# A spectral layer beside a Mish MLP: a shorter reciprocal root on VectorE, and a few tiles and reductions in other slots

## The chip, the cores and the metric

One core of a Trainium2 chip runs the whole program. The metric is device time in microseconds of one execution. TensorE (PE) multiplies matrices into PSUM, VectorE (DVE) and ScalarE (ACT) work on rows, GpSimd (POOL) does some of the subtractions, and SyncE (SP) issues the transfers.

## The reference, cut to what matters

```python
x = A_x                                   # (1, 2048, 512)
xn = layernorm(x)                         # eps 1e-5
X = rfft2(xn) * (w_r + 1j * w_i)          # spectral branch
y = irfft2(X, s=(2048, 512))
h = xn @ w1 + b1                          # w1: 512 x 1792
act = h * tanh(softplus(h))               # Mish
out = x + y + act @ w2                    # w2: 1792 x 512
```

## The kernel before

The 2048 rows are cut into four groups of 512 rows, each of four blocks of 128 (block s of group g is called (g, s) here). Every matrix operand is split into a high and a low half of 16 bits, and a product is three matmuls (`mm3`: high by high, high by low, low by high; lines 86, 89, 90).

The MLP runs in half tiles. There are 56 tiles (g, f), four groups by 14 columns of 128. An *up tile* (`mlp_up`, PSUM tile `ph`, line 725) is twelve matmuls; ScalarE then applies Mish (`hb`, line 733), and ScalarE and VectorE split the result into halves (`a`, lines 334 and 335). A *down tile* (`mlp_down`, PSUM tiles `pa`) is twelve matmuls that add one tile to the group's four sums. After a group's 14 down tiles `mlp_end` reads the four sums out (`m`, line 779), which frees their PSUM for the next group's. `mlp_all` decides the order: as long as there are fewer than `lag` up tiles ahead of the down tiles, an up tile comes next, otherwise a down tile.

The spectral branch normalises each group (`stats`: line 176 to 180, then the reciprocal root `rsqrt_of`, then `norm`), transposes its blocks (`transpose`: tile `pt`, line 200, copied to `xnT` by VectorE in line 290 and ScalarE in line 291), and makes the first transform (`s1_forward`: `psS`, a butterfly `bt_s` on VectorE, a cast `y` on ScalarE and a subtraction on GpSimd, line 129). The result goes to DRAM and comes back turned (`p2_unit`, `psP`). Four spectra follow (`spectrum`): each has two pairs of PSUM tiles `psD` (`d_pair`), the product with the weights, and `psA`, `psT` with a second butterfly `bt_t`. `s1_inverse` (`psY`) ends it.

Tiles `pt` and `ph` share one pool of two PSUM buffers, in the order in which they are made. The spectral tiles `psS`, `psP`, `psD`, `psA`, `psT` and `psY` share another pool of two. The largest weight of the spectral product is found by eight reductions of 128 x 1024 and one of `w0` (`prep_spectral`, lines 458 and 467), then GpSimd takes the maximum over the partitions (`am`), and a scale `sc_u` is made of it.

Three tables set the order. Ahead of the stream there are numbered slots: each holds some pieces of work, and after each slot one half tile is issued. Then comes the stream of spectral work: each piece carries a weight, and half tiles are issued in proportion to the sum of weights (`B_END` and `N_WGT`). At last the 16 inverse blocks are spread over the half tiles left. A scheduler orders the instructions of neighbouring pieces by their priority, so that an engine's queue is not exactly the order of the code.

```python
lag = LEAD if sc["ahead"] else LAG
for k in range(13, 23):
    slots[k].append((next, maxima, None))
while done[0] - start < used * (B_END - start) / N_WGT and half_tile():
```

Of the kernel before, what the change touches and what calls it, by code (L numbers as in the profile page):

```python
# [19 lines left out]
P = 128  # L20
NS2 = 16
NFC = F // P
CONST_SCALE = 1024.0
LAG = 4
NA = 5
HB = 3
LEAD = 8
E_UP = 11
N_WGT = 117.6
B_END = 98  # L30
T_LAG = 4
T_HOLD = 2
# [7 lines left out]
def spectral_mlp_kernel(ctx, tc, x, wt, w0, w1, b1, w2, cT, cIT, cM, out):  # L40
    nc = tc.nc
# [3 lines left out]
    sp = ctx.enter_context(tc.tile_pool(name="sp", bufs=1))  # L45
# [96 lines left out]

    def rsqrt_of(g, ve):

        eng = nc.gpsimd if g else nc.vector
        r = sp.tile([P, 4], F32, tag="rr", name=f"rr_{g}_0", bufs=4)

        eng.tensor_scalar(
            r.bitcast(I32), ve.bitcast(I32), -0.5, float(0x5F3759DF), op0=ALU.mult, op1=ALU.add
        )  # L150
        for k in range(3):

            t = sp.tile([P, 4], F32, tag="rt", name=f"rt_{g}_{k}", bufs=2)
            eng.tensor_mul(t, r, r)
            q = sp.tile([P, 4], F32, tag="rq", name=f"rq_{g}_{k}", bufs=2)
            if g:

                eng.tensor_mul(q, t, ve)
                eng.tensor_scalar(q, q, 0.25**k, -3.0, op0=ALU.mult, op1=ALU.add)
            else:  # L160
                eng.scalar_tensor_tensor(q, t, 0.25**k, ve, op0=ALU.mult, op1=ALU.mult)
            n = sp.tile([P, 4], F32, tag="rr", name=f"rr_{g}_{k + 1}", bufs=4)
            if g:
                eng.tensor_mul(n, q, r)
            else:
                eng.scalar_tensor_tensor(n, q, 3.0, r, op0=ALU.subtract, op1=ALU.mult)
            r = n
        rs = sp.tile([P, 4], F32, tag="rs", name=f"rs_{g}", bufs=2)
        eng.tensor_scalar(rs, r, -128.0, None, op0=ALU.mult)
        return rs  # L170

    def stats(g, ts):
# [172 lines left out]
    sc = {}  # L345
# [421 lines left out]

    def rows_back(g):

        macc[g] = cp.tile([P, 4, D], F32, tag=f"xnT{g}", name=f"m_{g}")  # L770
        nc.sync.dma_start(macc[g], xv[:, 4 * g : 4 * g + 4, :])

    def mlp_end(g):
        if g == 3:
            macc[g] = cp.tile([P, 4, D], F32, tag=f"xnT{g}", name=f"m_{g}")
        m = macc[g]
        for s in range(4):
            xr = yacc[g][s] if g == 3 else m[:, s, :]
            nc.vector.scalar_tensor_tensor(m[:, s, :], pacc[g][s], sc["out"], xr, op0=ALU.mult, op1=ALU.add)  # L779
            if g == 3:  # L780
                nc.sync.dma_start(outv[:, 4 * g + s, :], m[:, s, :])

    def mlp_all():

        tiles = [(g, f) for g in range(4) for f in range(NFC)]
        acts = {}
        up = down = n_down = 0
        while down < len(tiles):
            lag = LEAD if sc["ahead"] else LAG

            home = sc["ahead"] and up % 12 > 3
            free = down >= up - up % 4 - 8 if home else len(in_a) < NA or in_a[-NA] < down
            if free and up < len(tiles) and (up < E_UP or up - down < lag or (n_down >= 2 and up - down > lag)):
                mlp_up(*tiles[up], acts)
                if tiles[up][1] == NFC - 1 and tiles[up][0] < 3:
                    rows_back(tiles[up][0])
                up += 1
                n_down = 0
            else:
                g, f = tiles[down]  # L800
                mlp_down(g, f, acts.pop((g, f)))
                if f == NFC - 1:
# [61 lines left out]
    def stream_a():  # L864

        todo = []

        def behind(n):
            if len(todo) > n:
                ip_unit(*todo.pop(0))  # L870
                yield 1.0

        for c in range(5):
            if c < 4:
                for g in range(0, 4, 2):
                    p2_unit(c, g)
                    p2_unit(c, g + 1)
                    yield 1.6
                    yield from behind(0)
            if c:  # L880
                for g in range(4):
                    dp_unit(c - 1, g)
                    todo.append((c - 1, g))
                    yield 0.8
                    yield from behind(4)
            if c < 4:
                for wgt in spectrum(c):
# [69 lines left out]
        nc.sync.dma_start(cMt[:, :O_ID], cM[:, :O_ID])  # L957


    slots = {k: [] for k in range(24)}  # L960
    for s in range(4):
        slots[1 + s].append((s1_forward, 0, s, xh[0, s]))
    for g in range(1, 4):
        k = 6 * g - 6
        slots[k].append((st_, g))
        if g < 3:
            slots[k + 2].append((load_, g + 1))
        for s in range(4):
# [213 lines left out]
```

## Time and profile before

| | us |
|---|---|
| median of 3 runs | 400.26 (399.61 to 400.28) |
| profiled execution | 399.53 |
| its span | 397.7 |
| TensorE busy | 381.7 (96%) |
| VectorE busy | 250.8 (63%) |
| ScalarE busy | 200.9 (51%) |
| GpSimd busy | 69.7 (18%) |

The span runs from the first to the last instruction of the profiled execution. An engine that is busy 96% of it leaves little idle time; where that lies, and what ended it, is in the rows further down.

### The profile page before, as it was taken

The numbers are of one execution on the slowest core, as the hardware profiler recorded it, in microseconds if no ns is written. First come the engines' busy times: TensorE is split into PE (matmuls) and PEld (weight loads), VectorE is DVE, ScalarE is ACT, GpSimd is POOL, SyncE is SP. The second block draws the span as 40 slices with busy tenths as digits, with TensorE's granted clock in tenths as the row PEclk, the third lists the DMA queues.
The fourth block names the chain that finished last, engine by engine and source line by source line (L and its number), as shares of the span: only waits on it lengthen the run. The fifth ranks groups of instructions, "written<-read, shape, count | busy, mean of one in ns | idle before, by whom it ended". The sixth has DMA issues, their size and how long they took to land.

```text
span 397.7 us, 6578 instructions
## 1 busy us (share of the span) xinstructions
PE 381.7 (96%) x2485; PEld 191.4 (48%) x2485; DVE 250.8 (63%) x520; ACT 200.9 (51%) x325; POOL 69.7 (18%) x103
## 2 busy tenths in 40 slices
PE   8899999699998999999999999999999899999996
PEld 3444444345454454465445565455654445544442
DVE  5889777658697339843879446944439872424334
ACT  3869863576655155734646355365454474523110
POOL 0100029557565000000111101021001110220000
PEclk9999999999999999999999999999999999999999
DMA  8996015254186970353825625227471022753556
GB/s 281 363 396 258 2 53 158 81 166 151 55 297 188 271 228 3 79 134 98 255 73 144 175 54 164 77 87 200 166 190 50 27 81 70 215 171 114 173 196 253
DMA packets 49519, 61.61 MB, mean 155 GB/s; under 512 B 3776, under 2 KB 36032, under 8 KB 48848
## 3 DMA queue, kind: packets, MB, share of 16 engines
q1 hardware_dynamic: 49488, 61.20, 49.6%
q8 instruction: 19, 0.31, 0.3%
q14 instruction: 12, 0.10, 0.1%
HBM read 44.38 MB, written 16.78 MB: 154 GB/s over the span
## 4 chain that ended last, share of the span: by engine, by line
PE 54%; DVE 7%; ACT 2%; issue 2%; DMA 1%; POOL 1%; POOLq 0%; DVEq 0%; SPq 0%; ACTq 0%
PE ph L725 20%; PE pa L86 8%; PE pa L89 8%; PE pa L90 7%; PE psD L544 3%; PE psP L520 3%; DVE m L779 2%; PE psY L86 1%; PE psY L90 1%; PE psY L89 1%; PE psA L86 1%; POOL tt L129 1%; DVE a L335 1%; DMA yi<-d_t 1%; PE psA L90 1%
## 5 line engine op out<-in xcount | busy, mean ns | idle before, releaser
L725 PE MATMUL ph<-xnT,w1t 128*128 128x512 f16 x672 | 154.3, 379 | 1.9 <-ACT xnT L291 0.9
L725 PEld LDWEIGHTS <-w1t 128*128 128x128 f16 x672 | 64.7, 98 | 79.1 <-issue 2.4
L86 PE MATMUL pa<-w2r,a 128*128 128x512 f16 x224 | 84.4, 380 | 1.6 <-DVE m L779 1.4
L89 PE MATMUL pa<-w2r,a 128*128 128x512 f16 x224 | 85.0, 379 | 0.5 <-DVE w2r L335 0.5
L90 PE MATMUL pa<-w2r,a 128*128 128x512 f16 x224 | 85.0, 379 | 0.0
L335 DVE SCALAR_TENSOR_TENSOR a<-hb,sc_a,a 128x512 f16<-128x512 f32 x56 | 42.5, 761 | 56.7 <-ACT a L334 56.4
L733 ACT ACTIVATE hb<-ph,b1t,sc_exp 128x512 f32<-128x512 f32 x56 | 43.2, 771 | 59.5 <-PE ph L725 59.4
L129 POOL TENSOR_TENSOR tt<-bt_t,tt 128x512 f16<-128x512 f32 x16 | 19.6, 1230 | 195.8 <-ACT tt L128 152.9
L334 ACT ACTIVATE a<-hb,sc_a 128x512 f16<-128x512 f32 x56 | 40.1, 720 | 1.5
L90 PEld LDWEIGHTS <-a 128*128 128x128 f16 x224 | 21.9, 98 | 26.8 <-issue 1.1
L89 PEld LDWEIGHTS <-a 128*128 128x128 f16 x224 | 21.9, 98 | 25.7 <-issue 1.9
L86 PEld LDWEIGHTS <-a 128*128 128x128 f16 x224 | 21.9, 98 | 25.8 <-issue 1.2
L334 ACT ACTIVATE u<-r,sc_u 128x512 f16<-128x512 f32 x16 | 11.5, 721 | 25.3 <-DVE r L624 12.6
L129 POOL TENSOR_TENSOR y<-bt_s,y 128x512 f16<-128x512 f32 x16 | 20.1, 1261 | 18.2 <-ACT y L128 18.2
L833 DVE SCALAR_TENSOR_TENSOR m<-psY,sc_k,m 128x512 f32<-128x512 f32 x12 | 8.7, 747 | 14.9 <-PE psY L90 14.9
L128 ACT CAST tt<-bt_t 128x512 f16<-128x512 f32 x16 | 9.9, 617 | 14.9 <-DVE bt_t L126 13.4
L679 DVE SCALAR_TENSOR_TENSOR at<-psA,at 128x512 f16<-128x512 f32 x16 | 10.8, 689 | 10.4 <-ACT at L678 10.4
L128 ACT CAST y<-bt_s 128x512 f16<-128x512 f32 x16 | 9.9, 617 | 14.5 <-DVE bt_s L126 7.8
L556 ACT ACTIVATE ix<-psD 64x512 f32<-64x512 f32 x16 | 9.5, 593 | 12.8 <-PE psD L544 12.6
L678 ACT ACTIVATE at<-psA 128x512 f16<-128x512 f32 x16 | 9.2, 591 | 12.5 <-issue 7.1
L194 POOL TENSOR_TENSOR xh<-xs,xh 128x512 f16<-128x512 f32 x12 | 14.4, 1217 | 3.9 <-ACT xh L193 3.9
L544 PE MATMUL psD<-z,cMt 64*128 64x256 f16 x192 | 13.5, 270 | 1.5 <-DVE bt_t L126 1.5
(146 smaller groups left out, 510.1 us busy)
## 6 DMA issues: line engine op xcount, KB each, us to landing
wt<-in_wt_dram SPq DMA_DIRECT2D x32, 256.0 KB
x<-in_x_dram SPq DMA_DIRECT2D x8, 512.0 KB
d_y<-y SPq DMA_DIRECT2D x16, 256.0 KB
wm<-in_wt_dram SPq DMA_DIRECT2D x8, 512.0 KB
yt<-d_y SPq DMA_DIRECT2D x16, 256.0 KB
d_a<-at SPq DMA_DIRECT2D x32, 128.0 KB
ai<-d_a SPq DMA_DIRECT2D x16, 256.0 KB
d_t<-tt SPq DMA_DIRECT2D x16, 256.0 KB
```

What stands on the lines that cost most here:

```text
L86: first = nc.tensor.matmul(ps, stat(0), mov(0), start=start, stop=False)
L89: nc.tensor.matmul(ps, stat(0), mov(1), start=False, stop=False)
L90: return nc.tensor.matmul(ps, stat(1), mov(0), start=False, stop=stop)
L128: nc.scalar.copy(out[:, :, 0, :], tv)
L129: nc.gpsimd.tensor_sub(out[:, :, 1, :], tv, out[:, :, 0, :])
L194: nc.gpsimd.tensor_sub(xh[:, 1, :], xs, xh[:, 0, :])
L334: hi = nc.scalar.activation(dst_h, src, AF.Copy, scale=scale)
L335: lo = nc.vector.scalar_tensor_tensor(dst_l, src, scale, dst_h, op0=ALU.mult, op1=ALU.subtract)
L520: first = nc.tensor.matmul(ps[64 * be : 64 * be + 64, pr, k, :], yt[:, 2 * pr + be, hs, k, :], c_p2[:, k, v, hm, :], start=t == 0, stop=t ...
L544: first = nc.tensor.matmul(ps[be][:, k], c_d[rows, k0 + k, e, hs, :], z[rows, hm, 2 * (k0 + k) + e].rearrange("p g q -> p (g q)"), start=e ...
L725: last_mm = nc.tensor.matmul(ph, w1t[:, hs, dc, f * P : (f + 1) * P], xnT[g][:, hm, dc, :], start=n == 0, stop=n == 11)
L733: nc.scalar.activation(hb, ph, AF.Mish, bias=b1t[:, f : f + 1], scale=s_exp[k])
```

## The change

- The reciprocal root of a group's variances now takes eight VectorE instructions besides the one that adds the epsilon, in all four groups: a first value from the bits, one Newton step, and one step of higher order. Before, group 0 had eleven on VectorE and groups 1 to 3 had fourteen on GpSimd.
- The transposes of group 1 come one slot later, and the first up tile of group 1 (number 14 of all) waits until fewer than 6 up tiles are ahead, not 8.
- Two of the w2 splits come one slot earlier (slots 9 and 12 in place of 10 and 13).
- The ten steps of the search for the largest weight stand in slots 16 to 25 in place of 13 to 22. So there are 26 slots in place of 24, and two more half tiles are issued ahead of the stream.
- The end of a group counts 1.5 in the sum of weights, and the divisor goes from 117.6 to 120.6.

```diff
+LEAD_1 = 6
-N_WGT = 117.6
+N_WGT = 120.6
...
     def rsqrt_of(g, ve):
-        eng = nc.gpsimd if g else nc.vector
...
-        for k in range(3):
-            t = sp.tile([P, 4], F32, tag="rt", name=f"rt_{g}_{k}", bufs=2)
-            eng.tensor_mul(t, r, r)
-            q = sp.tile([P, 4], F32, tag="rq", name=f"rq_{g}_{k}", bufs=2)
-            if g:
-                eng.tensor_mul(q, t, ve)
-                eng.tensor_scalar(q, q, 0.25**k, -3.0, op0=ALU.mult, op1=ALU.add)
-            else:
-                eng.scalar_tensor_tensor(q, t, 0.25**k, ve, op0=ALU.mult, op1=ALU.mult)
...
+        v = nc.vector
+        v.tensor_scalar(r.bitcast(I32), ve.bitcast(I32), -0.5, float(0x5F3759DF), op0=ALU.mult, op1=ALU.add)
+        v.tensor_mul(t, r, r)
+        v.scalar_tensor_tensor(q, t, -192.0, ve, op0=ALU.mult, op1=ALU.mult)
+        v.scalar_tensor_tensor(n, q, 576.0, r, op0=ALU.add, op1=ALU.mult)
+        v.tensor_mul(t, n, n)
+        v.scalar_tensor_tensor(w, t, 384.0**-2, ve, op0=ALU.mult, op1=ALU.mult)
+        v.scalar_tensor_tensor(p, w, -10.0 / 3, w, op0=ALU.add, op1=ALU.mult)
+        v.scalar_tensor_tensor(rs, p, 5.0, n, op0=ALU.add, op1=ALU.mult)
...
     def mlp_end(g):
+        sc["ended"] = 1.5
...
-            lag = LEAD if sc["ahead"] else LAG
+            lag = (LEAD if up != NFC else LEAD_1) if sc["ahead"] else LAG
...
-            slots[k + 6 + s].append((t_, g, s))
+            slots[k + 6 + s + (g == 1)].append((t_, g, s))
...
-        slots[(1, 4, 7, 10, 13, 15)[c - 1]].insert(0, (split_w2, c))
-    for k in range(13, 23):
+        slots[(1, 4, 7, 9, 12, 15)[c - 1]].insert(0, (split_w2, c))
+    for k in range(16, 26):
         slots[k].append((next, maxima, None))
...
-        used += wgt
+        used += wgt + sc.pop("ended", 0.0)
```

How the instructions move on two engines, in three places. VectorE at group 1's first transposes, before: `st`, `mv` and `ve` are group 2's statistics, `pt_762` holds the transposes of block (1, 0), `a_12` is up tile (0, 12), `pt_848` the transposes of (1, 1).

```order
L190 TENSOR_SCALAR xs_787<-x_1_124,mv_568,rs_602 128x512
L176 BN_STATS st_791<-x_1_662 128x6 x2
L178 BN_AGGR mv_792<-st_791 128x2 x4
L180 TENSOR_SCALAR ve_801<-mv_792 128x4
L290 COPY xnT_761<-pt_762 128x4x128
L125 SCALAR_TENSOR_TENSOR bt_s_4_780<-psS_4_773,bc_s_4_778 128x4x64
L126 SCALAR_TENSOR_TENSOR bt_s_4_780<-psS_4_773,bc_s_4_778 128x4x64
L335 SCALAR_TENSOR_TENSOR a_12_843<-hb_12_841,sc_a,a_12_843 128x512
L290 COPY xnT_761<-pt_848 128x4x128
```

VectorE at the same place now (`pt_800` holds the transposes of (1, 0)):

```order
L173 BN_AGGR mv_752<-st_751 128x2 x4
L175 TENSOR_SCALAR ve_761<-mv_752 128x4
L149 TENSOR_SCALAR rr_0_763<-ve_761 128x4
L151 TENSOR_TENSOR rt_0_765<-rr_0_763 128x4
L153 SCALAR_TENSOR_TENSOR rq_0_767<-rt_0_765,ve_761 128x4
L155 SCALAR_TENSOR_TENSOR rr_1_769<-rq_0_767,rr_0_763 128x4
L158 TENSOR_TENSOR rt_1_771<-rr_1_769 128x4
L160 SCALAR_TENSOR_TENSOR rq_1_773<-rt_1_771,ve_761 128x4
L162 SCALAR_TENSOR_TENSOR rt_2_775<-rq_1_773 128x4
L164 SCALAR_TENSOR_TENSOR rs_777<-rt_2_775,rr_1_769 128x4
L330 SCALAR_TENSOR_TENSOR a_12_794<-hb_12_792,sc_a,a_12_794 128x512
L285 COPY xnT_799<-pt_800 128x4x128
```

The eight steps of group 2's root and the split of up tile (0, 12) now stand ahead of the first copy of group 1. On TensorE that up tile comes ahead of the transposes of (1, 0) in place of behind them, and a down tile stands between the transposes of (1, 0) and (1, 1).

VectorE at the end of group 0, before: `mxw` are the reductions of the search, `m` the four sums, `a_4` is up tile (1, 4).

```order
L467 TENSOR_REDUCE mxw<-w0t 128x1
L335 SCALAR_TENSOR_TENSOR a_4_1407<-hb_4_1405,sc_a,a_4_1407 128x512
L290 COPY xnT_1279<-pt_1410 128x4x128
L125 SCALAR_TENSOR_TENSOR bt_s_15_1428<-psS_15_1421,bc_s_15_1426 128x4x64
L126 SCALAR_TENSOR_TENSOR bt_s_15_1428<-psS_15_1421,bc_s_15_1426 128x4x64
L458 TENSOR_REDUCE mxw<-wm_1350 128x1
L779 SCALAR_TENSOR_TENSOR m_931<-pa_0_604,s_out,m_931 128x512
L779 SCALAR_TENSOR_TENSOR m_931<-pa_3_607,s_out,m_931 128x512
L458 TENSOR_REDUCE mxw<-wm_1389 128x1
L469 TENSOR_REDUCE mxwa<-mxw 128x1
```

VectorE at the same place now (sums 1 and 2 of the four are left out in both):

```order
L126 SCALAR_TENSOR_TENSOR bt_s_15_1386<-psS_15_1379,bc_s_15_1384 128x4x64
L127 SCALAR_TENSOR_TENSOR bt_s_15_1386<-psS_15_1379,bc_s_15_1384 128x4x64
L453 TENSOR_REDUCE mxw<-wm_1308 128x1
L775 SCALAR_TENSOR_TENSOR m_883<-pa_0_589,s_out,m_883 128x512
L775 SCALAR_TENSOR_TENSOR m_883<-pa_3_592,s_out,m_883 128x512
L453 TENSOR_REDUCE mxw<-wm_1347 128x1
L453 TENSOR_REDUCE mxw<-wm_1392 128x1
L453 TENSOR_REDUCE mxw<-wm_1411 128x1
L462 TENSOR_REDUCE mxw<-w0t 128x1
L330 SCALAR_TENSOR_TENSOR a_5_1461<-hb_5_1459,sc_a,a_5_1461 128x512
L453 TENSOR_REDUCE mxw<-wm_1430 128x1
L464 TENSOR_REDUCE mxwa<-mxw 128x1
```

Before, seven reductions and that of `w0` stand ahead of the four sums and one behind them; now four stand ahead, and four and that of `w0` behind.

TensorE at the second pair of the last spectrum, before: `ph_4` is up tile (3, 4), `psD_2_1` and `psD_2_0` are the pair.

```order
L725 MATMUL ph_4_3793<-xnT_1279,w1t 128x512
L544 LDWEIGHTS cMt
L544 MATMUL psD_2_1_3812<-z_3308,cMt 128x256
L544 LDWEIGHTS cMt
L544 MATMUL psD_2_0_3811<-z_3308,cMt 128x256
```

TensorE at the same place now (`pa_0` and `pa_1` are sums of down tile (3, 1)):

```order
L91 MATMUL psT_3762<-ai_3760,cMt 128x256
L539 LDWEIGHTS cMt
L539 MATMUL psD_2_1_3779<-z_3275,cMt 128x256
L87 LDWEIGHTS a_1_3589
L87 MATMUL pa_0_3726<-w2r,a_1_3589 128x512
L90 MATMUL pa_0_3726<-w2r,a_1_3589 128x512
L91 MATMUL pa_0_3726<-w2r,a_1_3589 128x512
L87 MATMUL pa_1_3727<-w2r,a_1_3589 128x512
L90 MATMUL pa_1_3727<-w2r,a_1_3589 128x512
L91 MATMUL pa_1_3727<-w2r,a_1_3589 128x512
L539 LDWEIGHTS cMt
L539 MATMUL psD_2_0_3778<-z_3275,cMt 128x256
```

Six matmuls of a down tile now stand between the first matmuls of the pair's two tiles, and the transform `psT` stands behind the up tile in place of ahead of it.

## Rows read from the trace of the kernel before

**Rows 1.** The page: busy time, share of the span, instructions of each engine.
```profile
PE 381.7 (96%) x2485; PEld 191.4 (48%) x2485; DVE 250.8 (63%) x520; ACT 200.9 (51%) x325; POOL 69.7 (18%) x103
```

**Rows 2.** Stretches: from:to, length, each engine's busy us (instructions), clock, DMA share, GB/s.
```profile
60.00:92.00 32.00, 27.47 (x155) 13.22 (x154) 21.32 (x39) 17.17 (x30) 20.64 (x28) 1.00 0.47 148
92.00:132.00 40.00, 38.63 (x222) 19.09 (x221) 32.40 (x58) 22.48 (x40) 23.26 (x36) 1.00 0.56 180
132.00:300.00 168.00, 167.50 (x1352) 89.30 (x1351) 100.22 (x226) 86.15 (x143) 10.71 (x9) 1.00 0.49 137
300.00:322.00 22.00, 20.55 (x118) 10.19 (x117) 18.94 (x42) 10.46 (x17) 3.55 (x3) 1.00 0.10 37
```

**Rows 3.** TensorE's timeline, its gaps: start, us, instruction, [idle before <-releaser].
```profile
63.59 0.38 PE L89 MATMUL pa<-w2r,a 128*128 128x512 f16 x1 [0.45 <-DVE w2r L335]
...
72.56 0.61 PE L200 MATMUL pt<-cMt,xh 128*128 128x128 f16 x8 [2.75 <-ACT xnT L291]
...
78.18 1.02 PE L725 MATMUL ph<-xnT,w1t 128*128 128x512 f16 x4 [0.68 <-ACT xnT L291]
...
84.99 0.39 PE L725 MATMUL ph<-xnT,w1t 128*128 128x512 f16 x1 [0.38 <-DVE xnT L290]
85.65 2.53 PE L725 MATMUL ph<-xnT,w1t 128*128 128x512 f16 x11 [0.26 <-ACT xnT L291]
...
128.31 0.38 PE L86 MATMUL pa<-w2r,a 128*128 128x512 f16 x1 [1.37 <-DVE m L779]
...
317.20 1.05 PE L544 MATMUL psD<-z,cMt 64*128 64x256 f16 x16 [1.45 <-DVE bt_t L126]
```

**Rows 4.** TensorE's timeline, transposes of (1, 0) and up tile (0, 12).
```profile
65.96 0.61 PE L200 MATMUL pt<-cMt,xh 128*128 128x128 f16 x8
...
67.06 2.32 PE L725 MATMUL ph<-xnT,w1t 128*128 128x512 f16 x10
```

**Rows 5.** VectorE's timeline, 65 to 72 us.
```profile
65.89 1.36 DVE L190 TENSOR_SCALAR xs<-x,mv,rs 128x512 f32<-128x512 f32 x1 [1.05 <-POOL xh L194]
...
71.17 0.40 DVE L180 TENSOR_SCALAR ve<-mv 128x4 f32<-128x4 f32 x1
71.48 0.41 DVE L290 COPY xnT<-pt 128x512 f16<-128x512 f16 x1
```

**Rows 6.** GpSimd's and VectorE's timeline, 55 to 61 us: group 1's root.
```profile
55.61 0.20 POOL L148 TENSOR_SCALAR rr<-ve 128x4 int32<-128x4 int32 x1 [11.96 <-DVE ve L180]
...
59.56 0.25 POOL L169 TENSOR_SCALAR rs<-rr 128x4 f32<-128x4 f32 x1
59.79 1.16 POOL L129 TENSOR_TENSOR y<-bt_s,y 128x512 f16<-128x512 f32 x1
...
60.98 0.42 DVE L125 SCALAR_TENSOR_TENSOR bt_s<-psS,bc_s 128x256 f32<-128x256 f32 x1 [1.56 <-POOL y L129]
```

**Rows 7.** VectorE's and ScalarE's timeline at the end of group 0's root.
```profile
9.37 0.17 DVE L169 TENSOR_SCALAR rs<-rr 128x4 f32<-128x4 f32 x1
...
9.70 0.18 ACT L377 ACTIVATION_READ_ACCUMULATOR w1t<-w1s 128x1 f32 x1
9.79 0.80 ACT L227 ACTIVATE xh<-x,nb,rs 128x512 f16<-128x512 f32 x1
```

**Rows 8.** VectorE's timeline, the reduction ahead of group 0's sums.
```profile
126.38 1.21 DVE L458 TENSOR_REDUCE mxw<-wm 128x1 f32<-128x1024 f32 x1
```

**Rows 9.** VectorE's and ScalarE's timeline: the scale made, and first used.
```profile
135.41 0.15 DVE L297 TENSOR_SCALAR cl_W<-am 128x1 f32<-128x1 f32 x1 [3.86 <-POOL am L471]
...
156.09 0.72 ACT L334 ACTIVATE u<-r,sc_u 128x512 f16<-128x512 f32 x1 [3.56 <-DVE r L627]
```

**Rows 10.** Line 647: count, ns min/median/max, first and last; then the timeline at 301 us.
```profile
L647 DVE TENSOR_TENSOR r<-g,c0t x8: 271/282/1129, 154.0 to 312.2; 4x128 f32<-4x128 f32 x8
...
301.30 1.23 POOL L129 TENSOR_TENSOR tt<-bt_t,tt 128x512 f16<-128x512 f32 x1 [27.85 <-ACT tt L128]
301.54 1.13 DVE L647 TENSOR_TENSOR r<-g,c0t 4x128 f32<-4x128 f32 x1
```

More of the change, by code (lines that the diff above doesn't have):

```diff
@@ L143, in rsqrt_of @@
     def rsqrt_of(g, ve):
-        eng = nc.gpsimd if g else nc.vector
         r = sp.tile([P, 4], F32, tag="rr", name=f"rr_{g}_0", bufs=4)
-        eng.tensor_scalar(
-            r.bitcast(I32), ve.bitcast(I32), -0.5, float(0x5F3759DF), op0=ALU.mult, op1=ALU.add
-        )
-        for k in range(3):
-            t = sp.tile([P, 4], F32, tag="rt", name=f"rt_{g}_{k}", bufs=2)
-            eng.tensor_mul(t, r, r)
-            q = sp.tile([P, 4], F32, tag="rq", name=f"rq_{g}_{k}", bufs=2)
-            if g:
-                eng.tensor_mul(q, t, ve)
-                eng.tensor_scalar(q, q, 0.25**k, -3.0, op0=ALU.mult, op1=ALU.add)
-            else:
-                eng.scalar_tensor_tensor(q, t, 0.25**k, ve, op0=ALU.mult, op1=ALU.mult)
[L162 to L167, printed above, removed]
+        v = nc.vector
+        v.tensor_scalar(r.bitcast(I32), ve.bitcast(I32), -0.5, float(0x5F3759DF), op0=ALU.mult, op1=ALU.add)
+        t = sp.tile([P, 4], F32, tag="rt", name=f"rt_{g}_0", bufs=2)
+        v.tensor_mul(t, r, r)
+        q = sp.tile([P, 4], F32, tag="rq", name=f"rq_{g}_0", bufs=2)
+        v.scalar_tensor_tensor(q, t, -192.0, ve, op0=ALU.mult, op1=ALU.mult)
+        n = sp.tile([P, 4], F32, tag="rr", name=f"rr_{g}_1", bufs=4)
+        v.scalar_tensor_tensor(n, q, 576.0, r, op0=ALU.add, op1=ALU.mult)
+        t = sp.tile([P, 4], F32, tag="rt", name=f"rt_{g}_1", bufs=2)
+        v.tensor_mul(t, n, n)
+        w = sp.tile([P, 4], F32, tag="rq", name=f"rq_{g}_1", bufs=2)
+        v.scalar_tensor_tensor(w, t, 384.0**-2, ve, op0=ALU.mult, op1=ALU.mult)
+        p = sp.tile([P, 4], F32, tag="rt", name=f"rt_{g}_2", bufs=2)
+        v.scalar_tensor_tensor(p, w, -10.0 / 3, w, op0=ALU.add, op1=ALU.mult)
         rs = sp.tile([P, 4], F32, tag="rs", name=f"rs_{g}", bufs=2)
-        eng.tensor_scalar(rs, r, -128.0, None, op0=ALU.mult)
+        v.scalar_tensor_tensor(rs, p, 5.0, n, op0=ALU.add, op1=ALU.mult)
         return rs
@@ L957, in matrices @@
         nc.sync.dma_start(cMt[:, :O_ID], cM[:, :O_ID])
-    slots = {k: [] for k in range(24)}
+    slots = {k: [] for k in range(26)}
     for s in range(4):
@@ L987, in spectral_mlp_kernel @@
     start, used = done[0], 0.0
+    sc.pop("ended", None)
     for wgt in stream_a():
-        used += wgt
+        used += wgt + sc.pop("ended", 0.0)
         while done[0] - start < used * (B_END - start) / N_WGT and half_tile():
```

## The prediction

> **What bounds the kernel now.** I read the page first, then stretches of the run, then TensorE's own gaps, then the engine that ends each gap. The first line of the page is to be read as a bound: TensorE is busy 381.7 us of a span of 397.7 [rows 1], and the clock is 1.00 in every stretch [rows 2], so 16.0 us of idle TensorE is all that an edit of the order can win. The stretches say where these lie. Between 132 and 300 us TensorE idles 0.5 us in 168; from 60 to 92 it idles 4.5 us, from 92 to 132 1.4, from 300 to 322 1.5 [rows 2]; the 8.1 left lie before 60 and after 322, at the start and the end, where the change moves little. TensorE's own rows then give the gaps one by one with who ended them [rows 3]: 0.45 (the low half of a w2 block), 2.75 (a transpose that waits for the copy of the transpose before it), 0.68, 0.38 and 0.26 (up tiles that wait for copies), 1.37 (group 1's sums wait for group 0's to be read), 1.45 (the second spectral pair waits for a butterfly). Sum 7.34.
>
> **Why the 2.75 us are there.** Transposes and up tiles share two PSUM buffers. Before, the order is transposes of (1,0), its spectral matmuls, up tile (0,12), transposes of (1,1). The third user needs the first one's buffer, so the copy of (1,0) must be done within one up tile: ten of its matmuls take 2.32 with the last 0.38 long, so 0.216 apart and 2.59 for twelve [rows 4]. But VectorE is in group 2's statistics: its queue has the last two normalisations and eight short steps ahead of the copy, which starts at 71.48, 5.6 us after the queue went busy at 65.89 following a wait for GpSimd [rows 5]. That wait is itself late GpSimd work: the root of group 1 holds GpSimd from 55.61 to 59.81, the first subtraction starts only at 59.79, and VectorE sits 1.56 us for it before 60.98 [rows 6].
>
> **The change part by part.**
> Root. In group 0 eleven VectorE steps become eight besides the one that adds the epsilon, three fewer at about 0.20 each (9.37 to the next, 9.57), 0.6 us. I cost the gain at 0.0 to 0.1: ScalarE is inside the sum of squares of w1 until 9.88 and starts the scaling at 9.79, 0.05 after VectorE is done with the bias [rows 7]. In groups 1 to 3 fourteen GpSimd steps, 4.2 us per group, leave GpSimd; eight steps come to VectorE, 8 x 0.20 = 1.6 us where they stand in one dependent run, about 1 us where butterflies lie between. What it gives: the 1.56 wait goes, so the w2 block behind it ends about 1.5 earlier and TensorE's 0.45 gap closes. Below: 0; above: 0.45. I take 0.45, as 1.5 is three times the gap.
> Transposes of group 1 one slot later, up tile (1,0) held. Now the PE order is up tile (0,12), transposes (1,0), the three spectral matmuls, twelve matmuls of a down tile, transposes (1,1), three more, up tile (0,13). The buffer that (1,1) takes is the up tile's, read by ScalarE long before; the copy of (1,0) is due at up tile (0,13). By TensorE that is: down tile ends 65.5 (0.45 earlier), + 2.59 up, + 1.10 for transposes and spectral matmuls (65.96 to 67.06, rows 4), + 2.59 down, + 1.10 = 72.9. By VectorE: the statistics ended 71.5 [rows 5]; less 1.56 and less the 1.05 wait gives 68.9; + 1.6 for the root, + 0.7 for a split, + 0.4 for the copy, + 0.6 for ScalarE's half = 72.2. So 0.7 us of room: the 2.75 go. The same arithmetic one turn on (w2 split 1.2, butterfly 0.7, two copies 1.0) puts the copy of (1,1) at 74.8 and its user at 75.5. Up tile (1,0) now stands behind the transposes of (2,0) and two down tiles (5.2 us) after the last copy of group 1, so 0.68, 0.38 and 0.26 go too. Bounds 0.7 (below, rival A) and 4.07; I take 4.07.
> Price of it: transposes (2,0) to (2,3) now have an up tile between each, where before one pair had a down tile, and the root stands there too. I get room of 0.15 to 0.5 us at the three turns; nothing hides what runs over. Bounds 0 and 2.0; I take 0.6.
> Maxima three slots later. Four of eight 1.21 us reductions and the one of w0 move behind group 0's four sums [rows 8]; one still stands directly ahead, and the three nearest before it stay. The sums start when the butterfly and that one reduction are done. So of the 1.37 I take 0.8, bounds 0 and 1.37. The scale that the maxima feed begins to be worked out at 135.4 and is first used at 156.1 [rows 9]; they end about 4 us later against TensorE's place, and two half tiles (5.2 us) come between, so 20 us of room hide it. Descriptors: the weight loads keep their number; the first read-back stands ahead of them on SyncE, the other three behind them, and their users come about 9 us after TensorE's first spectral product: nothing.
> Group ends weighed, N_WGT 120.6. Two half tiles run before the stream instead of in it, one each from the second and third spectrum, and one half tile is drawn to the group's end. At the last spectrum the second pair's first matmul is followed by six matmuls of a down tile (1.30 us) before the second, which waits for the butterfly: 1.45 becomes about 0.15. Bounds 0 and 1.45, I take 1.3. What is lost is 5.2 us of cover for the chain through ScalarE, VectorE and DRAM in 168 us in which TensorE idles 0.5: bounds 0 and 5.2 + 4.35 (rival B), taken 0.5, since that row says that the cover was ample.
> **Sum.** 0.45 + 4.07 + 0.8 + 1.3 + 0.05 - 0.6 - 0.5 = 5.6 us. The profiled execution took 399.53 (span 397.7 and 1.8 around it), so 393.9. It lies 0.7 under the median of the three runs, 400.26, at their low end (399.61); for a median I add 0.5: **394.4 us**.
>
> **A rule weighed.** The rows show a 4-partition product on VectorE at 0.28 us (median of eight), but once at 1.13, when a GpSimd subtraction of 1.23 us had begun at 301.30, 0.24 before it [rows 10]. The Trainium skill (SBUF — State Buffer, "Who interferes with whom") says that a VectorE instruction with two SBUF inputs contends with a GpSimd instruction that reads SBUF and that the loser fully blocks until the other is done. By that rule, the row agrees; it speaks against moving the root, since its products have two such inputs and stand amid GpSimd subtractions. The sum by it would be rival A's.
>
> **Rivals.**
> A, the wait changes hands: the copy, not the buffer, was the cause, and VectorE now carries the root ahead of it. One or two of the eight steps meet a subtraction and grow by 0.85 each (1.13 - 0.28, rows 10), and the 1.05 wait for GpSimd stays. Then the copy of (1,0) ends at 72.2 + 1.05 + 1.7 = 75.0 against 72.9: up tile (0,13) waits 2.1 of the 2.75 removed, and group 2's turns lose their room, 1.0 instead of 0.6: 394.4 + 2.5 = 396.9. For it: the normalisations of 1.36 in [rows 5]. Against: GpSimd has 4.2 us less to do there, so the subtractions come earlier.
> B, slower: the stream, not TensorE, sets the pace. Place: the four spectra. With one half tile fewer in two of them, the second pair of each waits for the butterfly as at 317.20 now: four times 1.45 less the one there is, 4.35, and the cover lost comes back as 5.2. Early gains 0.45 + 4.07 + 0.8 = 5.3: 399.5 - 5.3 + 5.2 + 4.35 = 403.7, about 404 as a median. It decides once TensorE's idle in the stream exceeds the early gain, some 6 us against 2 now. For: VectorE busy 18.9 of 22 us at 300 to 322. Against: 0.5 us in 168 [rows 2].
> C, only the cover comes back: 399.5 - 5.3 + 5.2 = 399.4, about 400 as a median, no change.
> That the held tile does nothing is excluded by the order: it moves behind two down tiles.
>
> **How the numbers follow.** Forecast 0.65 with its own range 392.4 (all gaps gone, nothing lost) to 396.0; A 0.20; C 0.06; B 0.09. Faster by over 0.2% (about what a measurement of this kernel tells from no change) is the forecast and A, 0.85; same C, 0.06; slower B, 0.09. The range goes to 399.0, past A and towards C, and leaves out B and most of C.
>
> **What would show it.** Right: no TensorE gap over 0.3 us from 60 to 92; GpSimd's busy time 12 us lower; VectorE's wait for its subtraction gone at 60.98; idle of 0.3 to 0.7 ahead of group 1's first sums, under 0.4 ahead of the last second pair; the stream from first spectral product to last inverse still near full. Wrong: a gap ahead of up tile (0,13) or a transpose of group 2 ended by xnT (A); several gaps before psD or psA (B, C).

## The result: 0.5% slower, and the profile after

The changed kernel took 401.99 us (median of 7 runs, 400.70 to 403.44), the kernel before 400.17 (median of 7). The ratio is 1.0050, 95% interval 1.0030 to 1.0069: slower, where 394.4 us and a range up to 399.0 were forecast. The profiled execution is the longest of the seven, 403.44 us with a span of 401.7; that of before, 399.53, is shorter than any of its seven. So the traces lie 4.0 us apart in span, the medians 1.8.

The page after, busy time of each engine (answers to [rows 1]):

```profile
PE 384.9 (96%) x2485; PEld 192.0 (48%) x2485; DVE 255.7 (64%) x541; ACT 201.7 (50%) x325; POOL 59.2 (15%) x61
```

TensorE does the same 2485 matmuls and is busy 3.2 us longer; it idles 16.8 us where it idled 16.0. So 3.2 of the 4.0 us are longer busy time of the same matmuls (run 2 below puts 2.65 us down to the clock), and the idle time, which the change was forecast to cut by 5.6, did not fall. GpSimd is 10.5 us less busy (12 were forecast).

The stretches after (from:to, length, busy us of PE, PEld, DVE, ACT, POOL, granted clock, DMA share, GB/s; answers to [rows 2]):

```profile
60.00:92.00 32.00, 30.15 (x168) 14.64 (x167) 26.85 (x54) 18.34 (x31) 17.87 (x14) 1.00 0.48 141
92.00:132.00 40.00, 36.61 (x197) 17.84 (x197) 24.27 (x56) 22.16 (x39) 14.65 (x14) 0.91 0.47 154
132.00:300.00 168.00, 165.56 (x1341) 87.90 (x1340) 103.29 (x222) 82.86 (x136) 12.09 (x16) 1.00 0.50 139
300.00:322.00 22.00, 22.00 (x116) 10.65 (x116) 20.69 (x50) 12.01 (x21) 2.82 (x2) 1.00 0.20 64
```

Idle TensorE: 1.9 us from 60 to 92 (4.5 before), 3.4 from 92 to 132 (1.4 before, and the clock is 0.91), 2.4 from 132 to 300 (0.5 before), none from 300 to 322 (1.45 before). The early gain came; it was given back at once in the next stretch, and in the stream. Ahead of 60 us TensorE idles 0.25 more and behind 322 us 0.65 more than before; the prediction looked for little there.

TensorE's gaps after (start, us, instruction, idle before it and who ended it; answers to [rows 3]):

```profile
74.66 2.75 PE L720 MATMUL ph<-xnT,w1t 128*128 128x512 f16 x12 [1.07 <-ACT xnT L286]
...
93.69 0.61 PE L195 MATMUL pt<-cMt,xh 128*128 128x128 f16 x8 [2.38 <-ACT xnT L286]
...
96.19 5.28 PE L720 MATMUL ph<-xnT,w1t 128*128 128x512 f16 x12 [1.25 <-ACT hb L728]
...
131.07 0.38 PE L87 MATMUL pa<-w2r,a 128*128 128x512 f16 x1 [0.46 <-DVE m L775]
...
199.81 0.20 PE L87 MATMUL psT<-ai,cMt 128*128 128x64 f16 x1 [0.94 <-DMA ai<-d_a]
...
218.93 1.48 PE L539 MATMUL psD<-z,cMt 64*128 64x256 f16 x23 [0.78 <-DVE bt_t L127]
```

The 2.75 us ahead of the transposes of (1,1) are gone, with 1.07 at up tile (0,13) behind them. New are 2.38 ahead of the transposes of (2,1) and 1.25 ahead of up tile (1,1), 3.63 us within 5 us. The twelve matmuls at 96.19 then take 5.28 us where twelve take 2.75. Short stretches of 2 us show why (same columns):

```profile
92.00:94.00 2.00, 0.32 (x6) 0.31 (x6) 1.86 (x11) 0.87 (x2) 0.43 (x1) 1.00 0.84 282
94.00:96.00 2.00, 0.94 (x9) 0.42 (x7) 1.48 (x8) 1.15 (x2) 0.46 (x1) 0.81 0.22 66
96.00:98.00 2.00, 1.81 (x5) 0.71 (x5) 1.07 (x3) 1.13 (x3) 0.70 (x1) 0.50 0.16 51
...
102.00:104.00 2.00, 2.00 (x13) 0.98 (x11) 0.93 (x2) 1.30 (x3) 0.00 (x0) 0.98 0.24 75
```

TensorE was busy 0.32 us of the two from 92 to 94; the granted clock then fell to 0.50, which is 1.2 of 2.4 GHz, and stayed there until shortly after 102.

Why the copy of (2,0) was late: VectorE's timeline ahead of it.

```profile
81.30 1.28 DVE L330 SCALAR_TENSOR_TENSOR w2r<-w2r,sc_w 128x1024 f16<-128x1024 f32 x1
...
83.17 0.53 DVE L185 TENSOR_SCALAR xs<-x,mv,rs 128x512 f32<-128x512 f32 x1
...
84.41 2.18 DVE L330 SCALAR_TENSOR_TENSOR w2r<-w2r,sc_w 128x1024 f16<-128x1024 f32 x1
...
87.65 2.66 DVE L185 TENSOR_SCALAR xs<-x,mv,rs 128x512 f32<-128x512 f32 x2 [0.39 <-POOL xh L189]
90.23 2.46 DVE L171 BATCH_NORM_STATS2 st<-x 128x6 f32<-128x512 f32 x4
92.61 0.40 DVE L285 COPY xnT<-pt 128x512 f16<-128x512 f16 x1
```

and GpSimd's beside it:

```profile
84.36 1.16 POOL L130 TENSOR_TENSOR y<-bt_s,y 128x512 f16<-128x512 f32 x1 [4.32 <-ACT y L129]
...
88.69 1.34 POOL L130 TENSOR_TENSOR y<-bt_s,y 128x512 f16<-128x512 f32 x1
```

The transposes of (2,0) were done at 88.07 (PE, 87.21 + 0.86). The copy stood behind group 2's last two normalisations, 1.33 us each, and all four statistics of group 3. Then ScalarE's half (93.05) lets the transposes of (2,1) go, and the activation of up tile (1,0), queued on ScalarE behind that copy, starts at 95.37 and lets up tile (1,1) go at 96.19. In this trace both waits stand behind the one late copy; run 5 below shows that the second stays when the copy comes early.

In the kernel before, one of the four statistics stood ahead of that copy, and the transposes of (2,1), at 94.29 us, did not wait:

```profile
92.24 0.69 DVE L176 BATCH_NORM_STATS2 st<-x 128x6 f32<-128x512 f32 x1
92.84 0.41 DVE L290 COPY xnT<-pt 128x512 f16<-128x512 f16 x1
93.17 0.69 DVE L176 BATCH_NORM_STATS2 st<-x 128x6 f32<-128x512 f32 x1
```

An up tile stood between the transposes of (2,0) and (2,1) there too. What is new on TensorE is the up tile (1,1) between (2,1) and (2,2), where a down tile stood.

### The profile page after: what moved, and what is told of

Read it like the earlier page. It is cut to its first block, busy times and chain, and to the rows that moved or that the text cites. A ratio compares the mean times of both kernels' runs of the same rounds, so it can differ in the third digit from the quotient of the medians.

```text
span 401.7 us, 6553 instructions
## 1 busy us (share of the span) xinstructions
PE 384.9 (96%) x2485; PEld 192.0 (48%) x2485; DVE 255.7 (64%) x541; ACT 201.7 (50%) x325; POOL 59.2 (15%) x61
## 4 chain that ended last, share of the span: by engine, by line
PE 57%; DVE 15%; issue 8%; ACT 8%; DMA 6%; POOL 4%; SPq 1%; POOLq 0%; DVEq 0%; ACTq 0%
PE ph L720 21%; PE pa L87 8%; PE pa L90 8%; PE pa L91 8%; PE psD L539 3%; PE psP L515 2%; ACT hb L728 2%; POOL xh L189 2%; ACT a L329 2%; DMA w1s<-in_w_dram 2%; DMA ai<-d_a 2%; POOL y L130 2%; DVE a L330 2%; DVE m L775 1%; ACT w1t L329 1%
## 5 line engine op out<-in xcount | busy, mean ns | idle before, releaser
L720 PE MATMUL ph<-xnT,w1t 128*128 128x512 f16 x672 | 156.2, 384 | 2.9 <-ACT hb L728 1.3
L528 DVE SCALAR_TENSOR_TENSOR z<-psP,z 128x512 f16<-128x512 f32 x16 | 10.7, 688 | 6.7 <-ACT z L527 6.7
L551 ACT ACTIVATE ix<-psD 64x512 f32<-64x512 f32 x16 | 9.5, 593 | 10.8 <-PE psD L539 10.5
L204 PE MATMUL ps_warm<-warm 128*128 128x512 f16 x47 | 13.6, 447 | 1.2 <-DVE warm L199 1.2
```

The costliest lines, as they stand in the source:

```text
L204: nc.tensor.matmul(ps, warm[:, 0:P], warm, start=True, stop=True)
L720: last_mm = nc.tensor.matmul(ph, w1t[:, hs, dc, f * P : (f + 1) * P], xnT[g][:, hm, dc, :], start=n == 0, stop=n == 11)
```

## Experiments

Times are medians; the ratio is to the kernel before on the same chip, with its 95% interval. Its median was 400.30 beside runs 1 to 4, 400.29 beside 5 to 8, 399.94 beside 9 to 12 and 399.91 beside 13. Runs 1 to 8 ran on one chip and 9 to 13 on another, where the kernel before is 0.35 us faster, so across these two groups only the distance to the kernel before compares. Run 4's redundant matmuls write a result again; no run leaves anything out.

| run | kernel | us | ratio |
|---|---|---|---|
| 1 | changed, no held tile | 398.26 | 0.9950 (0.9938 to 0.9962) |
| 2 | changed, root of before | 401.14 | 1.0027 (1.0013 to 1.0041) |
| 3 | before + late part | 401.18 | 1.0025 (1.0016 to 1.0034) |
| 4 | changed + 12 redundant matmuls | 403.63 | 1.0079 (1.0056 to 1.0103) |
| 5 | changed, group 3's statistics a slot later | 398.73 | 0.9958 (0.9944 to 0.9971) |
| 6 | run 1 without the late part | 397.32 | 0.9926 (0.9914 to 0.9939) |
| 7 | before + weighing | 399.67 | 0.9984 (0.9975 to 0.9993) |
| 8 | before + maxima later, 26 slots | 400.92 | 1.0010 (1.0000 to 1.0020) |
| 9 | before + root | 399.35 | 0.9985 (0.9976 to 0.9994) |
| 10 | before + shift of transposes and w2 splits | 396.90 | 0.9918 (0.9904 to 0.9931) |
| 11 | run 6 + weighing | 396.83 | 0.9916 (0.9903 to 0.9930) |
| 12 | run 11, group 2's statistics a slot later | 396.62 | 0.9910 (0.9897 to 0.9924) |
| 13 | run 11 with the root of before | 396.43 | 0.9911 (0.9897 to 0.9925) |

**Run 1, the held tile.**

```diff
-LEAD_1 = 6
+LEAD_1 = 8
```

> The changed kernel, but up tile (1,0) is not held (its limit is 8 again); all else of the change stays. Theory 1 (the held tile put up tiles between the transposes of group 2, and the ring of two PSUM buffers then waits for late copies, 2.38 and 1.25 us at 91 to 96 us, after which the clock falls and costs about 2.9 more): both waits go, the clock stays at 1.00 in every stretch, up tile (1,0) waits about 1.3 for copies again: 402.0 - 3.6 - 2.9 + 1.3 = 396.8. Rival 2 (VectorE is late there whatever TensorE's order, because the root and four statistics stand ahead of the copy): a wait of 2 us or more for the copy of the transposes of (2,0) stays, and so does the clock's fall: 401 to 402.

Measured 398.26, 3.7 less than the changed kernel, the clock at 1.00 in all five runs. TensorE's gaps from 73 to 100 us:

```profile
74.28 2.75 PE L720 MATMUL ph<-xnT,w1t 128*128 128x512 f16 x12 [1.09 <-ACT xnT L286]
...
83.72 0.39 PE L720 MATMUL ph<-xnT,w1t 128*128 128x512 f16 x1 [1.48 <-DVE xnT L285]
```

VectorE at the copy of (2,0):

```profile
91.08 0.42 DVE L285 COPY xnT<-pt 128x512 f16<-128x512 f16 x1
...
92.53 2.47 DVE L171 BATCH_NORM_STATS2 st<-x 128x6 f32<-128x512 f32 x4
```

Both waits at 91 to 96 are gone and the forecast 1.3 at up tile (1,0) is 1.48: theory 1. The time is 1.5 above the forecast 396.8. Other waits came back, 1.22 at group 1's first sums where the changed kernel had 0.46, and the forecast took the fall of the clock at 2.9, its price in the slowest of the seven runs; how the 1.5 divides was not measured. Undoing the hold has also put the statistics behind the copy, so this run alone can't tell the order on TensorE from the order on VectorE.

**Run 2, the root of before in the changed kernel.**

```diff
-        v = nc.vector
+        eng = nc.gpsimd if g else nc.vector
...
```

> The changed kernel with the root of before (eleven VectorE steps in group 0, fourteen GpSimd steps in groups 1 to 3). Theory 1 (held tile and transposes): the waits at 91 to 96 us and the clock's fall stay within 0.5 us of what they are, the 0.45 gap of the w2 block comes back: 402 to 402.5. Rival 2 (the root on VectorE makes the copies late): the 1.07 us wait at 74 goes, the waits at 91 to 96 shrink by 1.6 us or more, the clock does not fall: 397 to 398.5.

Measured 401.14 (400.12 to 403.28), a little under theory 1's 402 to 402.5 and far above rival 2's 398.5. The 1.07 at up tile (0,13) went and 0.72 at the w2 block came, but the two waits stayed at 2.38 and 1.20: rival 2 falls as the cause of them. The instructions of TensorE are in the same order as in the changed kernel, and in the profiled execution the clock did not fall:

```profile
93.18 0.61 PE L201 MATMUL pt<-cMt,xh 128*128 128x128 f16 x8 [2.38 <-ACT xnT L292]
95.63 2.75 PE L726 MATMUL ph<-xnT,w1t 128*128 128x512 f16 x12 [1.20 <-ACT hb L734]
...
128.15 0.38 PE L87 MATMUL pa<-w2r,a 128*128 128x512 f16 x1 [0.75 <-DVE m L781]
```

That prices the clock. From the start of up tile (1,1) to the first sum, less the wait ahead of that sum, it is 128.15 - 95.63 - 0.75 = 31.77 us here and 131.07 - 96.19 - 0.46 = 34.42 in the changed kernel: 2.65 us for the same 181 matmuls. The shorter wait ahead of the sums, 0.46 in place of 0.75, is 0.3 less.

**Run 3, the late part alone** (maxima in slots 16 to 25, 26 slots, weighing, divisor).

```diff
-    for k in range(13, 23):
+    for k in range(16, 26):
...
+        sc["ended"] = 1.5
```

> The kernel before with the late part alone: maxima three slots later, 26 slots, group ends weighed, divisor 120.6; root, held tile, transposes and w2 splits as before. Theory 1: the late part gains about 0.9 at the first sums of group 1 and 1.45 at the last second pair and gives back about 2 in the stream (idle from 132 to 300 us: 2.4 in the changed kernel, 0.5 before): 399.5 to 400.5. Rival 3 (the late part is what made it slower): 401.5 or more. As predicted blind (gain 0.8 + 1.3 - 0.5): 398.6.

Measured 401.18, above theory 1's interval and a little under rival 3's: the late part costs 0.9 by itself, where the prediction had a gain of 1.6. TensorE idles 2.1 us from 132 to 300 us, 0.5 before:

```profile
132.00:300.00 168.00, 165.88 (x1344) 88.29 (x1343) 102.95 (x225) 85.55 (x141) 12.11 (x16) 1.00 0.51 140
```

**Run 4, the first wait filled.**

```diff
-        mm3(ps, lambda h: cTt[:, s2, h, :], lambda h: xh[:, h, :], True, True)
+        for _ in range(5 if s2 == 8 else 1):
+            mm3(ps, lambda h: cTt[:, s2, h, :], lambda h: xh[:, h, :], True, True)
```

> The changed kernel with the first-step product of block (2,0) made five times instead of once into the same PSUM tile (12 redundant matmuls, 2.59 us, between the transposes of (2,0) and the up tile behind them). If the clock falls because TensorE stood idle for 3.6 of 5 us at 91 to 96: the redundant matmuls fill the 2.38 wait, the clock stays at 1.00, the up tile behind takes 2.75 instead of 5.28: 402.0 - 2.9 = about 399, with twelve matmuls more than the changed kernel. If the fall has another cause (the work done up to there, say): the clock still falls and the time is 402 to 404.6.

Measured 403.63 (401.53 to 405.32): my expectation missed. The fill took the 2.38 wait away, but the second wait grew:

```profile
96.64 4.42 PE L721 MATMUL ph<-xnT,w1t 128*128 128x512 f16 x12 [2.19 <-ACT hb L729]
```

Up tile (1,0) came later. Its activation (95.81) stood on ScalarE behind the same late copy (92.51) and behind the cast (95.29) that follows the butterfly of (2,0), and that butterfly (94.47) stood on VectorE behind all eight steps of group 3's root. The clock fell behind the 2.19 instead. So the test did not set idle against work done: with VectorE and ScalarE late, a fill on TensorE moved the wait. Of its six runs, the two at a clock of 0.999 and 1.000 took 401.5 and 402.3, the four at 0.994 to 0.996 403.4 to 405.3.

**Run 5, group 3's statistics one slot later.**

```diff
-        slots[k].append((st_, g))
+        slots[k + (g == 3)].append((st_, g))
```

> The changed kernel with one edit: the statistics of group 3 come one slot later (slot 13, not 12), so that VectorE's four statistics and the root of group 3 stand behind the copy of the transposes of (2,0) and not ahead of it. TensorE's order and the held tile stay. Theory 1a (the wait of 2.38 us is the queue on VectorE: four statistics, 2.4 us, ahead of the copy): the copy comes 2.4 us earlier, the waits of 2.38 and 1.25 us go below 0.5 each and the clock does not fall: 402.0 - 3.0 - 2 = 397. Rival (the held tile's order alone makes the ring too tight, or the two normalisations of 1.33 us and the split of 2.18 us beside GpSimd do): a wait of 1 us or more stays there, 400 or more.

Measured 398.73, 3.3 less, with the held tile in place and TensorE's order unchanged at this place (one matmul stands elsewhere, at 99.83 us). On VectorE the copy now follows the normalisations at once:

```profile
87.04 2.66 DVE L185 TENSOR_SCALAR xs<-x,mv,rs 128x512 f32<-128x512 f32 x2 [0.39 <-POOL xh L189]
89.62 0.41 DVE L285 COPY xnT<-pt 128x512 f16<-128x512 f16 x1
```

and on TensorE:

```profile
90.89 0.61 PE L195 MATMUL pt<-cMt,xh 128*128 128x128 f16 x8 [0.19 <-ACT xnT L286]
93.33 2.75 PE L720 MATMUL ph<-xnT,w1t 128*128 128x512 f16 x12 [1.20 <-ACT hb L728]
```

The 2.38 fell to 0.19: it was the four statistics. This gives back 3.3 of the 3.7 us that run 1 gave back. The second wait stayed, and the time is 1.7 above the forecast 397. Its end is ScalarE's queue (its activation at 92.51 stands behind the cast at 91.99, which follows the butterfly of block (2,0)); what would take it away was not tried. With 1.20 alone the clock stayed within 0.998 to 1.000 in all five runs.

**Runs 6 to 8, the late part taken apart.** Run 6 is run 1 with the maxima, slots and weights of before; run 7 adds to the kernel before the weighing alone, run 8 the slots alone (the hunks of run 3, one each).

> The changed kernel without the held tile and with the late part of before (maxima in slots 13 to 22, 24 slots, group ends not weighed, divisor 117.6): root, transposes and w2 splits of the change alone. Theory (the late part costs 0.9 by itself, as the late part alone showed on the kernel before): 398.26 - 0.9 = 397.4, stream idle below 1.0 us from 132 to 300, 1.45 back at the last second pair. Rival (the late part's 0.9 was the clock or chance): 398.3 or more, as the gain at the last pair is lost too.

> The kernel before with the weighing of group ends alone (1.5 each, divisor 120.6), 24 slots and maxima as before. If the loss of the late part comes from the two half tiles that the 26 slots take out of the stream: this one gains the 1.45 at the last second pair, 399.0 (range 398.7 to 399.5). If it comes from the weighing (one half tile fewer in the second and third spectrum): 400.5 to 401.

> The kernel before with the maxima three slots later and 26 slots alone, group ends not weighed. If the loss of the late part comes from the two half tiles fewer in the stream: 400.5 to 401.2, with 1.5 to 2 us of waits in the stream. If it comes from the weighing: 399.5 (0.8 gained at the first sums of group 1, nothing lost).

Run 6: 397.32, as forecast; the late part costs 0.9 beside the early part too. Run 7: 399.67, a gain of 0.6, just above the first forecast's 398.7 to 399.5: the 1.45 at the last second pair went, but 0.66 ahead of group 3's first sums came, and a transform's wait for DRAM grew from 0.33 to 0.75. Run 8: 400.92, a loss of 0.6 by the medians, though the interval of its ratio reaches 1.0000: the two half tiles that the 26 slots take out of the stream leave 1.8 us of idle from 132 to 300 (0.5 before), and the wait at group 1's first sums fell only from 1.38 (run 7) to 1.18.

```profile
132.00:300.00 168.00, 166.18 (x1346) 88.45 (x1344) 101.53 (x223) 85.02 (x139) 12.08 (x16) 1.00 0.51 139
```

Runs 7 and 8 do not add up to run 3: -0.6 and +0.6 alone, +0.9 together. Why they don't was not followed up.

Run 8 with run 3 shows one thing more. Run 8, the clock at 1.00:

```profile
73.00 0.61 PE L201 MATMUL pt<-cMt,xh 128*128 128x128 f16 x8 [2.75 <-ACT xnT L292]
78.64 2.75 PE L726 MATMUL ph<-xnT,w1t 128*128 128x512 f16 x12 [0.71 <-ACT xnT L292]
...
128.59 0.38 PE L87 MATMUL pa<-w2r,a 128*128 128x512 f16 x1 [1.18 <-DVE m L781]
```

Run 3, where the clock fell to 0.50 behind the same 2.75:

```profile
74.00:76.00 2.00, 2.00 (x6) 0.75 (x5) 0.00 (x0) 1.95 (x4) 1.50 (x8) 0.50 0.00 0
...
128.52 0.38 PE L87 MATMUL pa<-w2r,a 128*128 128x512 f16 x1 [1.19 <-DVE m L781]
```

Both reach the first sum at the same time: in run 3 the waits of 0.71, 0.39 and 0.27 that follow in run 8 are not there, the slower matmuls filled them. The kernel before has the same waits, and of its 23 runs beside runs 1 to 4 the 14 with a clock of 0.994 to 0.996 took no longer (399.96 to 400.47) than the 9 at 1.000 (400.10 to 400.53). Beside runs 5 to 8 the 12 with 0.994 to 0.996 took 400.02 to 400.88, the 8 with 0.998 to 1.000 399.86 to 400.56, and a single one with 0.991 took 402.49. These runs have no trace; that their clock fell behind the 2.75 is taken over from run 3.

**Runs 9 and 10, root and shift alone.** Run 9 adds the new root to the kernel before, run 10 the two lines of the shift:

```diff
-            slots[k + 6 + s].append((t_, g, s))
+            slots[k + 6 + s + (g == 1)].append((t_, g, s))
...
-        slots[(1, 4, 7, 10, 13, 15)[c - 1]].insert(0, (split_w2, c))
+        slots[(1, 4, 7, 9, 12, 15)[c - 1]].insert(0, (split_w2, c))
```

> The kernel before with the new root on VectorE alone. As predicted blind (the 0.45 gap at the w2 block goes, nothing lost): 399.8. Rival A of the prediction (the steps stand ahead of the copy of (1,0), whose wait is already 2.75 and grows): the wait ahead of the transposes of (1,1) grows to 3 us or more, 400.5 to 402, the more if the clock falls there.

> The kernel before with the transposes of group 1 one slot later and the two w2 splits one slot earlier, root, hold and late part as before. Theory (the shift is what gains, as run 6 with root and shift gained 3.0): the 2.75 wait goes, about 1.5 at up tile (1,0) comes in its place of 1.3 before, 397.2 to 397.8. If the gain of run 6 needed the root too: 398.5 or more.

Run 9: 399.35, the 0.45 gap gone and 0.6 gained, about as predicted; rival A's growth did not come (2.50 ahead of the transposes of (1,1), 2.75 before), since there the copy of (1,0) stands ahead of the root. Run 10: 396.90, 3.0 less and, with the 0.35 between the chips, at the lower end of its forecast, with 0.45 at the w2 block and 1.48 at up tile (1,0) left. Run 9's VectorE at group 1's root:

```profile
57.26 1.01 DVE L158 TENSOR_TENSOR rt<-rr 128x4 f32<-128x4 f32 x1
58.30 1.13 DVE L160 SCALAR_TENSOR_TENSOR rq<-rt,ve 128x4 f32<-128x4 f32 x1
...
60.41 0.42 DVE L126 SCALAR_TENSOR_TENSOR bt_s<-psS,bc_s 128x256 f32<-128x256 f32 x1
```

beside GpSimd there:

```profile
57.09 2.33 POOL L130 TENSOR_TENSOR y<-bt_s,y 128x512 f16<-128x512 f32 x2 [13.34 <-ACT y L129]
```

Two steps of 0.16 grew to 1.01 and 1.13 while GpSimd did its two subtractions (the second step ends at 59.43, the subtractions at 59.42), so the butterfly that stood at 60.98 [rows 6] came 0.57 earlier and not 1.56.

**Runs 11 to 13, towards a better version.** Run 11 is run 6 with the weighing, run 12 moves group 2's statistics a slot later (as run 5 did with group 3's), run 13 is run 11 with the root of before.

> Root, transposes, w2 splits and weighing of the change, without the held tile and with the maxima and slots of before. By the single parts: 397.32 (run 6) less 0.6 (run 7) = 396.7, with a wait of about 1.1 at up tile (0,13) and 1.5 at (1,0) left. If weighing and the rest do not add: 397.3.

> Run 11 with the statistics of group 2 one slot later (slot 7, not 6), so that the copy of the transposes of (1,0) stands ahead of the statistics and the root and not behind them. If VectorE's queue is what makes up tile (0,13) wait: the 1.08 wait goes, 395.6, lower than both kernels of the case. If the late statistics only move the wait to group 2's normalisations: 396.7 or more.

> Run 11 with the root of before: transposes one slot later, w2 splits one slot earlier, weighing of group ends, nothing else of the change. If the root on VectorE costs, where the shift is, what it gains at the w2 block (the copy of (1,0) then stands behind its eight steps): the 0.72 gap of the w2 block stands again, the 1.08 wait at up tile (0,13) goes, 396.2 (396.9 of run 10 less 0.6 of run 7). If the root gains by itself: 397.3.

Run 11: 396.83, near its forecast of 396.7. But that was worked out from run 6, on the other chip: against the kernel before, run 11 is 3.1 less and run 6 3.0, so the weighing gained 0.1 here and not 0.6 (runs 10 and 13, on one chip and with the old root, give 0.5). Run 12: 396.62, not 395.6: the 1.08 went, but 1.42 came ahead of the transposes of (1,2). VectorE's timeline in run 12 names the cause, the four statistics again, now ahead of the copy of (1,1):

```profile
73.87 2.46 DVE L171 BATCH_NORM_STATS2 st<-x 128x6 f32<-128x512 f32 x4
...
76.53 0.39 DVE L285 COPY xnT<-pt 128x512 f16<-128x512 f16 x1
```

Run 13: 396.43, near its forecast of 396.2. With the shift in place the root on VectorE gains nothing: by the medians of runs 11 and 13 it costs 0.4, by their ratios 0.2, and the intervals overlap. The traces show 1.08 at up tile (0,13) with it (run 11, first row) in place of 0.46 at the w2 block without it (run 13, second row):

```profile
74.15 2.75 PE L720 MATMUL ph<-xnT,w1t 128*128 128x512 f16 x12 [1.08 <-ACT xnT L286]
...
63.69 0.38 PE L90 MATMUL pa<-w2r,a 128*128 128x512 f16 x1 [0.46 <-DVE w2r L336]
```

Runs 10 to 13 beat the kernel before by 3.0 to 3.5 us and the changed kernel by more. Run 13, shift and weighing alone, has the lowest median; the four intervals overlap.

## Why the prediction was wrong

Taken one after the other, from the kernel before to the changed one, the parts are worth: -3.0 us for the shift (run 10), +0.1 to +0.4 for the root beside it (runs 6 and 10 across two chips, runs 11 and 13 on one), +0.9 for the late part (run 1 less run 6), +3.7 for the held tile (the changed kernel less run 1). These steps lead from one kernel to the other, so their sum meets the measured +1.8 by construction and tests nothing. Whether the parts add was seen only in part: the late part costs 0.9 on the kernel before (run 3) and 0.9 beside the shift, but the root gains 0.6 alone (run 9) and nothing beside the shift.

- **The step that failed: "Price of it: ... room of 0.15 to 0.5 us at the three turns; ... I take 0.6", with 2.0 as its upper bound.** The hold moved up tile (1,0) behind the transposes of (2,0), and with it all four statistics of group 3 came ahead of their copy in VectorE's queue. My room was counted for TensorE and the root; I left out of VectorE's queue what stands ahead of the copy of (2,0), four statistics (2.46) and two normalisations that take 1.33 each beside GpSimd and 0.53 alone. It cost 2.38 + 1.25 of waits, against the 0.6 taken. Run 5 shows the statistics to be the 2.38. The second wait is at the turn where a down tile stood before and now an up tile stands; it stays in run 5 at 1.20, and its end is ScalarE's queue.
- **What was not in the sum at all: the clock.** Some 2.65 us in the profiled execution, the slowest of the seven. Over the seven runs the granted mean goes from 0.998 (400.70) to 0.991 and 0.992 (402.82 and 403.44); a straight line through all seven reaches 400.3 at 1.00, an estimate that their scatter leaves uncertain by some 0.7. The profiled execution less 2.65, plus the 0.3 at the sums, would be 401.1. So by these estimates the changed kernel without the fall would stand level with the one before or up to 1 us behind, not ahead: the waits ate the gain, the clock made the loss or most of it.
- **The 4.07 of group 1's gaps** were nearly right: 2.75 + 0.68 + 0.38 + 0.26 went and 1.07 came. The 1.07 is rival A's wait, at the place that it named and half its size (2.1). Run 2 shows that it needs the root: without it the 1.07 is gone. The working by VectorE failed here: it had the statistics end at 68.9, and they ended at 71.42 (71.5 before): the 1.05 wait for GpSimd stayed, as rival A says, and the butterfly behind the old 1.56 wait stood at 60.99 (60.98 before). None of the eight steps grew there; each took 0.16 or 0.17.

```profile
65.73 1.36 DVE L185 TENSOR_SCALAR xs<-x,mv,rs 128x512 f32<-128x512 f32 x1 [1.05 <-POOL xh L189]
...
71.02 0.40 DVE L175 TENSOR_SCALAR ve<-mv 128x4 f32<-128x4 f32 x1
```

- **The root's 0.45** was right alone (run 9), by a smaller lead than worked out: 0.57 and not 1.56, because two steps met GpSimd's subtractions, as the rule weighed in the prediction says (the Trainium skill, SBUF — State Buffer, "Who interferes with whom"). The rule's mechanism held, the sum by it (rival A's) did not. The prologue term of 0.05 can't be seen: TensorE reaches its first wait for w1 at 28.83 to 29.11 us with the old root and at 28.85 to 29.51 with the new.
- **The maxima's 0.8** was mis-sized: 1.38 (run 7) became 1.18 by them alone (run 8). By run 8's VectorE the reduction that still stands directly ahead decides; the sums start behind it at 127.79:

```profile
126.67 1.21 DVE L459 TENSOR_REDUCE mxw<-wm 128x1 f32<-128x1024 f32 x1
```

- **The last pair's 1.3** was right at its place (1.45 gone, run 7), and most of it came back further on (0.66 and 0.42 there).
- **The cover's 0.5** was mis-sized: the stream's idle time grew by 1.3 from the slots alone (run 8), by 1.9 in the changed kernel, by the mechanism of rivals B and C but at about a fifth of B's 9.55. "That row says that the cover was ample" was the wrong reading: a row of 0.5 idle shows what is left over, not how much cover may go.

Rival B, slower, named the stream; the largest loss came at group 2's transposes. Both signs of rival A came, a gap ahead of up tile (0,13) and a transpose of group 2 ended by xnT, but only the first by its mechanism: the 2.38 stays without the root (run 2). So none of the rivals was the outcome.

What stays open: what decides whether the clock falls. Run 2's profiled execution had waits of 2.38 and 1.20 without a fall, the changed kernel's had the same waits with one, and run 2's twelve runs spread from 0.991 to 1.000. And not tried: the held tile with the ScalarE wait of run 5 removed.

## What to carry to other kernels

When a tile is moved to another turn of a small ring of buffers, list the whole in-order queue of the engine that empties the ring at the new place, statistics and normalisations included, before pricing the turn; otherwise the wait may only turn up elsewhere, as in runs 4 and 12. Price a long wait on TensorE (2.2 to 2.8 us here) also by the slower matmuls that may follow, unless later waits absorb them. A stretch with almost no idle time says nothing of how much cover it can lose.

## What the runs showed of the hardware

Behind a wait of 2.2 to 2.8 us the granted clock stood at 0.50 for some 3 to 7 us in the profiled executions of the changed kernel and of runs 3, 4 and 9, and stayed at 1.00 there in those of the kernel before and of runs 2, 7 and 8. That cost 2.65 us in the changed kernel, where TensorE then had no wait until the first sums at 131.07, and nothing by the first sums in run 3, where run 8 has waits of 0.71, 0.39 and 0.27 within some 13 us behind the fall. A VectorE step on 128x4 elements took 0.16 us alone and 1.01 to 1.13 beside a GpSimd subtraction of 128x512; a normalisation 0.53 alone and 1.33 beside GpSimd's subtractions, a w2 split 1.28 and 2.18.
